# Small expert products scheduled in halves of six matmuls, with new buffer hand-overs and a new order, in a fused attention and two-expert-layer kernel

## The chip, the cores and the metric

The kernel runs on one core of one Trainium2 chip. The metric is the device time of one execution in microseconds, the median of several executions. The engines are called PE (TensorE, matrix products), ACT (ScalarE), DVE (VectorE), POOL (GpSimd) and SP (SyncE, which starts most transfers). SBUF is the on-chip memory, PSUM the banks that PE writes its products to.

## What is computed

Attention of 4 x 8 heads over 576 positions with a decay, then two expert layers on its 2304 tokens of width 512, each with 2048 hidden columns:

```python
scores = scale * np.matmul(q, k.transpose(0, 1, 3, 2))
cum = np.cumsum(np.log(np.clip(f, 0.0001, 1.0)), axis=-1)
scores = np.where(causal, -1e9, scores + cum[..., :, None] - cum[..., None, :])
attn = exp(scores - max) ; attn = attn / (attn.sum(-1) + 1e-09)
x = (attn @ v), heads side by side                      # 2304 x 512
h = x @ w_in ; g = s * relu(h)**2 + b ; x = g @ w_out   # first layer
h = x @ w_in ; g = relu(h) + alpha * min(h, 0) ; out = g @ w_out   # second layer
```

## The kernel before

**Precision.** Matrix products that need it hold each operand as a high and a low part in a float32 form and run three passes: high by high, low by high, high by low (`PASSES`). So one product over 512 rows in chunks of 128 is 4 chunks x 3 passes = 12 matmuls.

**Stages.** Up to about 330 us attention runs beside the first layer's work on token blocks of 256 that are already complete ("small" expert products); from 330 to 590 us the first layer's remaining blocks run in pairs of 512 tokens ("big"); from 590 us the second layer runs, as seven products of blocks in place of eight. In the first stage PE does scores (L906, L907, and L911 for the first heads), transposes of the normalised rows (L1017, L981), value products (L1071), and for each hidden chunk `fc` of 128 the first expert product (L1121: 12 matmuls of 128x256 into bank `h`) and the second (L1153: 12 matmuls from `g` into two `a` banks, six each). Between the two stand ACT (L1131 relu), DVE (L1134 square), ACT (L1138 high part) and DVE (L1144 low part), in the functions `t_a`, `t_b`, `t_c`, `t_d`.

**Around the scores.** DVE masks a score bank and takes its row maximum (L919, followed by a read of an accumulator), ACT forms exponentials with row sums (L924, L927), DVE the reciprocals in two short steps (L931 and L932, or L934), POOL, ACT or DVE the division (L941 and L939). A *turn* is up to four transposes into one of two banks `t`. ACT or DVE evict them (L1026, L1028) into `pt`, from which the value products read; casts to a high part (L1077, ACT or DVE) and a low part (L1082) then make the token block `x`.

**Weights.** Expert weights arrive in packed words, are unpacked on DVE (L534, L537, L540), scaled by ACT (L543) and split into a high part (L560 on ACT, L564 on DVE) and a low part (L563 on POOL), into the tiles `i` (first product) and `o` (second).

**What sets the order.** The program is written as tasks with a list of engines on which each may run, an estimated duration, a priority, the keys it reads and writes, and the ring buffers that it uses. `Scheduler.run` plays these through a small model in time and starts on each engine the ready task with the lowest priority number whose buffers are to be had; the order in which tasks start is the order of the instructions on each engine. The priorities come from the table `PLAN`. A ring hands out a buffer when all users of an earlier one have ended. A *started* task only needs another to have been started ahead of it on the same engine.

**Second layer.** `second_layer` uses banks `h`, `k` and two `a` banks for first products (L1454), copies them out (L1469, L1471, L1492), forms `gq` and `gj` (L1494, L1377, L1379), and runs the second products into four banks `b` (L1392). Differences of token blocks, `xq`, are split on ACT (L1287) and DVE or POOL (L1286) into `xe`.

Of the kernel before, what the change touches and what calls it, by code (L numbers as in the profile page):

```python
# [50 lines left out]
    t0=3.26,  # L51
    ta=0.5395,
    tb=6.6087,
    t1=10.2011,
    t2=15.0154,
    t3=23.3962,
    prep=14.39,
    prepA=208.9144,
    nf=16,
    cp=7.3325,  # L60
    ip=-191.999,
    vp=-7.4436,
    mq=-6.3237,
    grp=4,
    grpA=3,
    max=2.3433,
    pv=3.6414,
    f2=-209.151,
    ap=-11.5752,
    c8=-13.6733,  # L70
    fo=0,
    kp=1,
    at=0,
    nrA='p',
    sc=0,
    wh=4,
    cd=-280.7657,
    ek=0,
    pa=4,
# [4 lines left out]
    xh='va',  # L84
# [3 lines left out]
    cv=(-18.0746, 6.2372, -68.3628, -99.9118, -31.1211, 35.9197, 230.8533, 210.2266, -6.9377, -5.1863, -34.7217, -80.0197, 0.8992, -68.8635, 81.6819, 79.6212),  # L88
    blocks=((-17.7552, 1.8684), (-0.719, 0.903), (0.4402, 2.1001), (1.1144, 1.9861), (1.7724, 2.5485), (2.9671, 3.0)),
# [16 lines left out]
class Buf:  # L106


    def __init__(self, ring):
        self.ring, self.users, self.t = ring, 0, None  # L110
# [16 lines left out]
class Scheduler:  # L127
# [8 lines left out]
    def task(self, opts, r=(), w=(), bufs=(), prio=0.0, started=()):  # L136
# [7 lines left out]
        t.bufs = tuple(bufs)  # L144
# [177 lines left out]
def dv(n):  # L322
    return 70 + 1.035 * n
# [30 lines left out]
def decay_attention_two_moe(ctx: ExitStack, tc: tile.TileContext, qk, qka, v, f, wi1, wo1, wi2, wo2,  # L354
# [14 lines left out]
    def ring(pool, tag, cap, shape, dt):  # L369
        return Ring(cap, lambda n: pools[pool][0].tile(shape, dt, tag=tag, bufs=cap, name=f"{tag}_{n}"))  # L370
# [44 lines left out]
    def o_at(n):  # L415
# [45 lines left out]
        "x": Ring(2, block(lambda i: f"x{i % 2}", "x", 4096 + 16, lambda i: 0 if i < 3 else 16 if i < 7 else 96, [P, KC, 2, T2], lambda i: i if i < 7 else None)),  # L461
# [527 lines left out]
    def transposes(u):  # L989
# [15 lines left out]
        for n, turn in enumerate(turns):  # L1005
            pr = u.t1 + (u.t1 - u.t0) * n / len(turns)
            pp, b0 = R["t"].buf(), 0
            for c, kbs in turn:
# [12 lines left out]
                for x, at, w in outs:  # L1021
                    def t_ev(copy, x=x, at=at, w=w, pp=pp, kbs=kbs, kw=kw, c=c, b0=b0):
# [4 lines left out]
                        else:  # L1027
# [3 lines left out]
                    task(pick(PLAN["ev"], a=("act", ac(nn), lambda f=t_ev: f(nc.scalar.copy)), v=("dve", dv(nn), lambda f=t_ev: f(nc.vector.tensor_copy))),  # L1031
                         r=[(K, "t", part)], w=[((owner, 0, c), "pt", part)], bufs=[pp, x], prio=pr)
                b0 += P * len(kbs)

# [71 lines left out]
    def moe_step(name, fc, x, x0, w, xk, acc, hring, first, last, pr1, pr2, epr, big, half=None):  # L1106
# [9 lines left out]
        def t_mm1():  # L1116
            wv = wi.t.rearrange("p l (k f) -> p l k f", k=KC)
            n = 0
            for kc in range(KC):
                for (wl, xl) in PASSES:  # L1120
                    nc.tensor.matmul(ps.t[:, 0:w], wv[:, wl, kc, :], x.t[:, kc, xl, x0:x0 + w], start=(n == 0), stop=(n == 3 * KC - 1))  # L1121
                    n += 1
# [25 lines left out]
        def t_mm2():  # L1148
            for u in range(KC):
# [8 lines left out]
        if half is None:  # L1158
            mms.append(task(("pe", 12 * mm, t_mm1), r=WK + xk, w=[(K, "h")], bufs=[ps, x, wi], prio=pr1))
# [30 lines left out]
        task(("pe", 12 * mm, t_mm2), r=[(K, "hi"), (K, "lo")] + OK, w=[AK], bufs=[g, wo] + acc, prio=pr2)  # L1190
        return AK

    def finish_pa(blk, acc, AK, epr):

        for i in range(2):
# [3 lines left out]
                 r=[AK, "p1"], w=[("pas", blk, i)], bufs=[acc[i], o], prio=epr)  # L1199
# [43 lines left out]
    def load_x(n, epr):  # L1243

        x = R["x"].buf()
# [9 lines left out]
    def second_layer(order, base, epr):  # L1255
# [3 lines left out]
        xa, xs_, xb = R["x"].buf(), R["xs"].buf(), R["x"].buf()  # L1259
# [7 lines left out]
        for n, (blk, rows) in enumerate(order):  # L1267
# [5 lines left out]
            for i, op in enumerate(XOPS):  # L1273
# [376 lines left out]
    def to_d():  # L1650
# [6 lines left out]
        S5.append(pools["px"][0].tile([P, TH], F32, tag="s5", bufs=1, name="s5_f"))  # L1657
    task(("py", 0.0, to_d), started=mid, w=["px"])
# [61 lines left out]
```

## Time and profile before

| | us |
|---|---|
| median of 3 runs | 947.12 |
| lowest and highest run | 946.66 and 948.70 |
| the profiled execution | 947.46 |
| its span, first to last instruction | 945.7 |
| PE busy | 932.2 |
| DVE, ACT, POOL busy | 711.5, 622.9, 336.6 |

The span is 1.8 us shorter than the profiled execution's own time; that part lies ahead of the first and behind the last instruction. A line such as L1121 is a line of the program before; after the change the same statement stands some 14 to 24 lines further down. PE's records of one operation overlap in the timeline because matmuls are pipelined; the start of the next row, and the idle time in brackets, tell when the engine had nothing to do. The DMA engines are busy 65% of the span, and no wait of PE names them.

### The profile page before, as it was taken

How to read it: one execution, taken by the hardware profiler on the slowest of the kernel's cores; microseconds unless marked ns; L12 is line 12 of the kernel's file. 1: busy time of each engine (PE TensorE's matmuls, PEld its weight loads, DVE VectorE, ACT ScalarE, POOL GpSimd, SP SyncE). 2: the span in 40 equal slices, each digit the busy share in tenths (PEclk: the TensorE clock that was granted, in tenths of full speed). 3: DMA queues.
4: the chain of work that ended last, by engine and by line, in shares of the span. 5: the costliest groups of instructions: out<-in, count | busy, mean ns of one | idle time of the engine just before them, and what ended most of it. 6: DMA issues, size and time to landing. Idle time of an engine off the chain costs nothing.

```text
span 945.7 us, 18349 instructions
## 1 busy us (share of the span) xinstructions
PE 932.2 (99%) x6342; PEld 842.6 (89%) x6342; DVE 711.5 (75%) x1554; ACT 622.9 (66%) x1457; POOL 336.6 (36%) x355
## 2 busy tenths in 40 slices
PE   9999999999999999999999999999999999999997
PEld 7578887999898888988888888999999999999997
DVE  8788858766677556575887675689986869778586
ACT  7799857756677567887777765566654456544552
POOL 7334402422133003577676742133241412523000
PEclk9999999999999999999999999999999999999999
DMA  7856416341534585676979584995698956889566
GB/s 204 268 153 228 148 48 192 124 125 57 189 90 142 179 242 161 226 260 221 361 252 352 198 272 154 352 330 184 188 318 254 320 168 181 254 255 318 164 187 204
DMA packets 99612, 201.41 MB, mean 213 GB/s; under 512 B 10832, under 2 KB 26032, under 8 KB 98880
## 3 DMA queue, kind: packets, MB, share of 16 engines
q1 hardware_dynamic: 99184, 199.78, 65.3%
q8 instruction: 50, 0.82, 0.4%
q10 hardware_dynamic: 336, 0.47, 0.2%
q14 instruction: 42, 0.34, 0.1%
HBM read 146.75 MB, written 50.51 MB: 209 GB/s over the span
## 4 chain that ended last, share of the span: by engine, by line
PE 90%; DVE 5%; ACT 3%; issue 1%; DMA 0%; ACTq 0%; POOL 0%; DVEq 0%; POOLq 0%
PE b L1392 16%; PE h L1121 14%; PE b L1156 9%; PE a L1153 9%; PE a L1454 8%; PE k L1121 6%; PE k L1454 5%; PE h L1454 5%; PE t L1071 4%; PE t L1017 3%; PE s L911 2%; PE a L1156 2%; PE s L906 2%; PE s L907 2%; ACT e L924 1%
## 5 line engine op out<-in xcount | busy, mean ns | idle before, releaser
L1392 PE MATMUL b<-wp,gj 128*128 128x256 f32 x1368 | 172.4, 278 | 0.8 <-DVE gj L1379 0.7
L1392 PEld LDWEIGHTS b<-wp,gj 128*128 128x128 f32 x1368 | 169.4, 188 | 1.2 <-DVE gj L1379 1.0
L1121 PE MATMUL h<-x,i 128*128 128x256 f32 (+1 forms) x864 | 146.4, 318 | 0.2 <-DVE r L1134 0.2
L1121 PEld LDWEIGHTS h<-x,i 128*128 128x128 f32 x864 | 124.4, 188 | 13.2 <-DVE r L1134 0.5
L1379 DVE TENSOR_TENSOR gj<-gq,gj 128x384 fp32r<-128x384 f32 x152 | 100.0, 667 | 31.6 <-ACT gj L1377 31.0
L1377 ACT CAST gj<-gq 128x384 fp32r<-128x384 f32 x142 | 73.0, 515 | 68.5 <-PE b L1392 64.3
L1153 PE MATMUL a<-g,o 128*128 128x256 f32 x768 | 101.3, 281 | 0.0
L1332 POOL TENSOR_TENSOR gq<-gq 128x384 f32<-128x384 f32 x33 | 39.6, 1200 | 162.3 <-DVE gq L1494 141.2
L1153 PEld LDWEIGHTS a<-g,o 128*128 128x128 f32 x768 | 94.7, 188 | 2.4 <-issue 1.0
L924 ACT ACTIVATE e<-e,ngm 128x256 f32<-128x256 f32 (+4 forms) x144 | 83.6, 582 | 19.1 <-DVE ngm L919 17.7
L941 POOL TENSOR_SCALAR e<-e,rec 128x128 f32<-128x128 f32 (+4 forms) x74 | 45.2, 622 | 138.7 <-DVE rec L934 49.1
L1156 PE MATMUL b<-g,o 128*128 128x512 f32 x384 | 93.8, 390 | 0.2 <-POOL g L1175 0.2
L1156 PEld LDWEIGHTS b<-g,o 128*128 128x128 f32 x384 | 71.5, 188 | 14.8 <-POOL g L1175 0.6
L1175 POOL TENSOR_TENSOR g<-r,g 128x512 fp32r<-128x512 f32 (+1 forms) x39 | 53.1, 1364 | 78.4 <-ACT g L1172 73.1
L919 DVE CUSTOM_DVE_ANT_0 e<-s,mask 128x256 f32<-128x256 f32 (+4 forms) x144 | 66.2, 478 | 15.6 <-PE s L907 10.8
L1131 ACT ACTIVATE r<-h 128x256 f32<-128x256 f32 (+1 forms) x76 | 34.0, 448 | 47.1 <-PE h L1121 46.0
L1017 PE MATMUL t<-ident,e 128*128 128x128 f32 (+1 forms) x376 | 54.6, 273 | 3.1 <-ACT pt L1028 2.2
L1454 PE MATMUL h<-x,wq 128*128 128x384 f32 x288 | 57.6, 335 | 0.0
L1017 PEld LDWEIGHTS t<-ident,e 128*128 128x128 f32 (+1 forms) x376 | 43.2, 139 | 11.9 <-issue 3.6
L534 DVE TENSOR_SCALAR cv<-raw 128x512 int32<-128x512 int32 x48 | 25.4, 528 | 37.2 <-ACT raw L543 28.3
L1454 PEld LDWEIGHTS h<-x,wq 128*128 128x128 f32 x288 | 49.4, 188 | 0.2
L1071 PE MATMUL t<-pt,v 128*64 128x320 f32 (+3 forms) x416 | 48.0, 368 | 0.3 <-ACT pt L1028 0.3
(197 smaller groups left out, 2020.2 us busy)
## 6 DMA issues: line engine op xcount, KB each, us to landing
wp<-w2o_d SPq DMA_DIRECT2D x168, 256.0 KB
wq<-w2i_d SPq DMA_DIRECT2D x112, 256.0 KB
raw<-in_wi_dram SPq DMA_DIRECT2D x29, 512.0 KB
w2o_d<-wq SPq DMA_DIRECT2D x56, 256.0 KB
w2i_d<-wq SPq DMA_DIRECT2D x56, 256.0 KB
raw<-in_wo_dram SPq DMA_DIRECT2D x27, 512.0 KB
rawqk<-in_qk_dram SPq DMA_DIRECT2D x20, 576.0 KB
v<-in_v_dram SPq DMA_DIRECT2D x20, 320.0 KB
```

The source lines that it names most:

```text
L919: nc.vector.tensor_tensor_reduce(e.t[0:rows, s0 + k0:s0 + k1], st_.t[0:rows, s0:s0 + w], mask[0:rows, m0:m0 + w], -0.125 if u.f32 else -1. ...
L924: nc.scalar.activation(x, x, AF.Exp, bias=ng[0:rows, col:col + 1], scale=-1.0, accum_out=sm[0:rows, col:col + 1])
L1017: nc.tensor.transpose(pp.t[0:kw, b0 + i * P:b0 + i * P + P], e.t[:, P * kb:P * kb + kw], ident)
L1071: nc.tensor.matmul(o.t[64 * j:64 * j + 64, a - q0:z - q0], vb.t[0:kr, kb, j, :], uu.pt[jj].t[0:kr, kb * step + a:kb * step + z], start=(i ...
L1121: nc.tensor.matmul(ps.t[:, 0:w], wv[:, wl, kc, :], x.t[:, kc, xl, x0:x0 + w], start=(n == 0), stop=(n == 3 * KC - 1))
L1153: nc.tensor.matmul(acc[u // 2].t[:, T * (u % 2):T * (u % 2) + T], wo.t[:, wl, u * P:u * P + P], g.t[:, gl, g0:g0 + w], start=(first and i ...
L1156: nc.tensor.matmul(acc[u].t[:, 0:w], wo.t[:, wl, u * P:u * P + P], g.t[:, gl, 0:w], start=(first and i == 0), stop=end)
L1175: eng.tensor_tensor(g.t[:, 1, g0:g0 + w], r_of(), g_hi().bitcast(F32), ALU.subtract)
L1377: task([("act", ac(TH, False), lambda g=g, qv=qv: nc.scalar.copy(g.t[:, 0, :], qv())), ("dvp", dv2(TH), lambda g=g, qv=qv: nc.vector.tenso ...
L1379: task(("dvp", dv(TH), lambda g=g, qv=qv: nc.vector.tensor_tensor(g.t[:, 1, :], qv(), g.t[:, 0, :].bitcast(F32), ALU.subtract)), r=[("G", ...
L1392: nc.tensor.matmul(y[t // 2].t[:, T * (t % 2):T * (t % 2) + T], g.t[:, gl, t * P:t * P + P], wop[k].t[:, wl, :], start=(fresh and k == 0 a ...
L1454: nc.tensor.matmul(b.t[:, 0:TH], wb.t[:, wl, k * P:k * P + P], x[:, k, xl, :], start=(start and m == 0), stop=(m == 5), skip_group_check=True)
```

## The change

1. **Halves.** A small product of a block of 256 tokens was one task of 12 matmuls. Each is now two tasks of six: the first product by chunks 0 and 1, then 2 and 3; the second product by its two `a` banks. The second task of a pair needs the first to have been started, and the scheduler may put other work between. The eviction of an `a` bank (`finish_pa`) waits for its own half.
2. **Turns.** The evictions of a turn were scheduled each when its own transposes were done; now they are scheduled when all transposes of the turn are done.
3. **Room of the token blocks.** The ring of two `x` buffers, one for a pair of blocks, becomes three: `x0` and `x0b`, which are the two halves of the first pair's buffer, and `x1`. Blocks 4 and 5 take over the room of blocks 0 and 1 one at a time. `Buf.more` lets a task that uses a whole pair count on both halves.
4. **Second layer.** The `xe` tiles are set up at one point, and the first step's casts into them get the lower urgency `epr + 0.5`, so that the copy out of bank `k` can come first.
5. **Order.** Nearly all numbers of `PLAN` are new: how groups of scores are formed (`grp`, `grpA`), when each stage's work falls due, and which engines may run some small steps.

```diff
 PLAN = dict(
-    grp=4,
-    grpA=3,
+    grp=2,
+    grpA=4,
-    pa=4,
+    pa=0,
-    nrA='p',
+    nrA='pv',
-    xh='va',
+    xh='a',
...
-        t.bufs = tuple(bufs)
+        t.bufs = tuple(bufs) + tuple(m for b in bufs for m in b.more if m not in bufs)
...
-        "x": Ring(2, block(lambda i: f"x{i % 2}", "x", 4096 + 16, ...)),
+    R["x0"] = Ring(1, x_even)
+    R["x0b"] = Ring(1, lambda n: xt[0] if n < 2 else "-")
+    R["x1"] = Ring(1, lambda n: x_of(2 * n + 1))
...
-                    task(pick(PLAN["ev"], a=..., v=...),
-                         r=[(K, "t", part)], w=[((owner, 0, c), "pt", part)], bufs=[pp, x], prio=pr)
+                    later.append((t_ev, nn, x, ((owner, 0, c), "pt", part)))
+                keys.append((K, "t", part))
                 b0 += P * len(kbs)
+            for t_ev, nn, x, key in later:
+                task(pick(PLAN["ev"], a=..., v=...),
+                     r=keys, w=[key], bufs=[pp, x], prio=pr)
...
-                X[blk] = R[{0: ...
+                X[blk] = R[{0: "x0", 1: "x0b", 2: "x1", 4: "x0", 5: "x0b", 6: "x1", 8: "xs"}[blk]].buf()
...
-            mms.append(task(("pe", 12 * mm, t_mm1), r=WK + xk, w=[(K, "h")], bufs=[ps, x, wi], prio=pr1))
+            if big:
+                task(("pe", 12 * mm, t_mm1), r=WK + xk, w=[(K, "h")], bufs=[ps, x, wi], prio=pr1)
+            else:
+                a = task(("pe", 6 * mm, lambda: t_mm1(range(0, 2))), r=WK + xk, w=[(K, "h0")], bufs=[ps, x, wi], prio=pr1)
+                task(("pe", 6 * mm, lambda: t_mm1(range(2, 4))), r=WK + xk, w=[(K, "h")], bufs=[ps, x, wi], prio=pr1, started=[a])
...
-        task(("pe", 12 * mm, t_mm2), r=[(K, "hi"), (K, "lo")] + OK, w=[AK], bufs=[g, wo] + acc, prio=pr2)
+        a = task(("pe", 6 * mm, lambda: t_mm2(range(0, 2))), r=[(K, "hi"), (K, "lo")] + OK, w=[(AK, 0)], bufs=[g, wo, acc[0]], prio=pr2)
+        task(("pe", 6 * mm, lambda: t_mm2(range(2, 4))), r=[(K, "hi"), (K, "lo")] + OK, w=[(AK, 1)], bufs=[g, wo, acc[1]], prio=pr2, started=[a])
...
-                 r=[AK, "p1"], w=[("pas", blk, i)], bufs=[acc[i], o], prio=epr)
+                 r=[(AK, i), "p1"], w=[("pas", blk, i)], bufs=[acc[i], o], prio=epr)
...
-                     w=[("xslot", i)], bufs=[b, xq], prio=pr)
+                     w=[("xslot", i)], bufs=[b, xq], prio=epr + 0.5 if n == 0 and i >= 5 else pr)
...
         S5.append(pools["px"][0].tile([P, TH], F32, tag="s5", bufs=1, name="s5_f"))
+        for n in range(NXE):
+            S5.append(pools["px"][0].tile([P, 2, 2, TH], F32R, tag=f"xe{n}", bufs=1, name=f"xe{n}_0"))
```

PE, the first small expert products, about 36 to 41 us of before. In the rows `h`, `s`, `t` and `a` are PSUM banks, `i` and `o` weight tiles, `lkx` the keys and queries of the first heads, `e` normalised rows, with running numbers behind the names. Before:

```order
L1121 MATMUL h_600<-x_428,i_0_501 128x256 x12
L911 MATMUL s_629<-lkx_326 128x384
L1017 MATMUL t_632<-ident,e_2_540 128x128 x4
L1017 MATMUL t_640<-ident,e_2_540 64x128
L1017 MATMUL t_640<-ident,e_4_553 128x128 x3
L1017 MATMUL t_658<-ident,e_4_564 128x128 x4
L911 MATMUL s_671<-lkx_326 128x512
```

Now:

```order
L1145 MATMUL h_505<-x_418,i_0_469 128x256 x3
L925 MATMUL s_587<-lkx_300 128x512
L1031 MATMUL t_592<-ident,e_3_530 128x128 x3
L1031 MATMUL t_600<-ident,e_3_543 128x128 x4
L1145 MATMUL h_505<-x_418,i_0_607 128x256 x3
L1171 MATMUL a_627<-g_612,o_0_564 128x256 x6
L925 MATMUL s_640<-lkx_325 64x288
```

The row of twelve is now two rows of three that stand apart, each on a different weight tile, with a score and seven transposes between; a half of a second product follows where transposes stood.

PE, the middle of attention, about 151 to 155 us of before (`pt` are evicted transposes, `v` values). Before:

```order
L906 MATMUL s_2159<-ka_2070,hq_2073 128x512
L907 MATMUL s_2159<-lk_2059 128x512
L1017 MATMUL t_2165<-ident,e_9_2056 128x128 x4
L1017 MATMUL t_2177<-ident,e_9_2056 64x128
L1017 MATMUL t_2177<-ident,e_18_2108 128x128 x3
L1017 MATMUL t_2194<-ident,e_7_2103 128x128
L1017 MATMUL t_2194<-ident,e_7_2105 128x128 x2
L1017 MATMUL t_2201<-ident,e_18_2127 128x128 x4
L1071 MATMUL t_2213<-pt_2117,v_1882 64x256
```

Now:

```order
L920 MATMUL s_2187<-ka_1843,hq_1872 64x288
L921 MATMUL s_2187<-lk_1841 64x288
L1140 MATMUL h_2199<-x_418,i_0_1506 128x256 x12
L1171 MATMUL a_2059<-g_2196,o_0_1500 128x256 x6
L1171 MATMUL a_2081<-g_2196,o_0_1500 128x256 x6
L920 MATMUL s_2239<-ka_1992,hq_2003 128x256
L921 MATMUL s_2239<-lk_1990 128x256
L1091 MATMUL t_2243<-pt_1968,v_1728 64x256
```

Before, a value product follows fifteen transposes; now twelve matmuls of a first product and two sixes of a second stand ahead of it instead, with a score between.

ACT at the start of the second layer, about 587 to 595 us of before, with the numbers of the tiles (`g2_55` is the first layer's last operand, `k_28`, `a_22`, `a_18`, `h_77`, `h_76` are banks). Before:

```order
L1172 ACTIVATE g2_55_7325<-r2_55_7232 128x512
L1287 CAST xe0_0_7386<-xq_0_6122 128x2x384
L1287 CAST xe1_0_7388<-xq_0_6122 128x2x384
L1471 COPY s5_f_7385<-k_28_7276 128x384
L1471 COPY u2_0_7398<-a_22_7270 128x384
L1492 ACTIVATE gq_0_7406<-h_77_7245,as_t_133 128x384
```

Now:

```order
L1194 ACTIVATE g2_55_7380<-r2_55_7286 128x512
L1494 COPY s5_f_7431<-k_28_7328 128x384
L1494 COPY u2_0_7435<-a_18_7318 128x384
L1515 ACTIVATE gq_0_7439<-h_76_7292,as_t_133 128x384
L1310 CAST xe0_0_7432<-xq_0_6157 128x2x384
L1310 CAST xe1_0_7433<-xq_0_6157 128x2x384
```

The two casts into `xe0` and `xe1` moved from ahead of the copies `s5_f` and `u2_0` to behind `gq_0`. PE at the same place, from the last row of the first layer, before:

```order
L1156 MATMUL b_11_7060<-g2_55_7325,o7_0_5935 128x512 x3
L1454 MATMUL k_28_7276<-xe0_0_7386,wq_90_7148 128x384 x6
L1454 MATMUL a_22_7270<-x_8_7230,wq_89_7145 128x384 x6
L1454 MATMUL h_77_7245<-x_7_6830,wq_91_7236 128x384 x6
L1454 MATMUL a_22_7270<-xe1_0_7388,wq_86_7089 128x384 x6
```

Now:

```order
L1174 MATMUL b_11_7095<-g2_55_7380,o7_0_6008 128x512 x3
L1477 MATMUL a_18_7318<-x_8_7284,wq_89_7191 128x384 x6
L1477 MATMUL h_76_7292<-x_7_6897,wq_91_7244 128x384 x6
L1477 MATMUL k_28_7328<-xe0_0_7432,wq_90_7199 128x384 x6
L1477 MATMUL a_19_7478<-xs_1_6989,wq_95_7362 128x384 x6
```

Bank `k` with `xe0` came first behind the first layer's last row; now bank `a` and bank `h`, each with a block that is not an `xe`, come ahead of it.

## Rows read from the trace of the kernel before

**Rows 1.** the page's busy times: engine, busy us (share of the span), instructions

```profile
PE 932.2 (99%) x6342; PEld 842.6 (89%) x6342; DVE 711.5 (75%) x1554; ACT 622.9 (66%) x1457; POOL 336.6 (36%) x355
```

**Rows 2.** busy us by stretch: length, each engine (instructions), clock, DMA

```profile
40.00:100.00 60.00, 59.24 (x415) 42.41 (x413) 51.10 (x146) 55.67 (x151) 22.23 (x20) 1.00 0.62 194
...
100.00:330.00 230.00, 226.82 (x1840) 202.59 (x1839) 164.98 (x511) 156.50 (x462) 60.02 (x90) 1.00 0.40 127
...
590.00:946.00 356.00, 349.59 (x2510) 348.09 (x2509) 280.55 (x529) 188.66 (x371) 88.99 (x78) 1.00 0.76 245
```

**Rows 3.** PE's waits: line <- what ended it: us, times, longest

```profile
PE s L911 <- DVE ngm L919: 2.4, 3, 1.3
PE t L1017 <- ACT pt L1028: 2.2, 4, 0.9
PE k L1454 <- ACT s_f L1471: 1.3, 1, 1.3
```

**Rows 4.** PE in order: start, us, operation, [idle before <- what ended it]

```profile
139.37 0.63 PE L1017 MATMUL t<-ident,e 128*128 128x128 f32 x4 [0.33 <-ACT pt L1028]
...
154.04 1.07 PE L1017 MATMUL t<-ident,e 128*128 128x128 f32 x7 [0.74 <-DVE pt L1028]
155.38 3.07 PE L1071 MATMUL t<-pt,v 128*64 128x256 f32 x28 [0.27 <-ACT pt L1028]
```

**Rows 5.** the same view, 36 to 50 us

```profile
36.91 0.91 PE L911 MATMUL s<-lkx 66*128 66x384 f32 x2 [0.52 <-DVE ngm L919]
...
39.27 0.63 PE L1017 MATMUL t<-ident,e 128*128 128x128 f32 x4 [0.58 <-ACT pt L1028]
...
49.02 1.19 PE L1121 MATMUL h<-x,i 128*128 128x256 f32 x8 [0.24 <-DVE r L1134]
```

**Rows 6.** the same view, 237 to 241 us

```profile
239.42 0.55 PE L1017 MATMUL t<-ident,e 128*128 128x128 f32 x3 [0.88 <-ACT pt L1028]
240.38 0.63 PE L1017 MATMUL t<-ident,e 128*128 128x128 f32 x4 [0.41 <-ACT pt L1028]
```

**Rows 7.** the chain that ended last: start, us, PE's expert matmuls

```profile
118.04 1.36 PE h L1121 x12
...
120.87 1.42 PE h L1121 x12
...
158.45 1.58 PE h L1121 x12
```

**Rows 8.** groups by shape, 0 to 330 us: busy, mean ns | idle before

```profile
L1134 DVE SCALAR_TENSOR_TENSOR r<-h,small,r 128x256 f32<-128x256 f32 x48 | 23.0, 479 | 16.1 <-ACT r L1131 15.6
...
L563 POOL TENSOR_TENSOR i<-cv,i 128x512 fp32r<-128x512 f32 x8 | 10.6, 1326 | 4.8 <-DVE i L564 3.4 <-ACT i L560 1.4
...
L931 DVE TENSOR_SCALAR rec<-sums 128x4 f32<-128x4 f32 x16 | 2.7, 168 | 7.9 <-ACT e L924 7.9
```

**Rows 9.** the start of the second layer, PE, ACT and POOL in order

```profile
594.47 1.31 PE L1454 MATMUL k<-xe,wq 128*128 128x384 f32 x6 [1.30 <-ACT s_f L1471]
...
593.21 0.83 ACT L1287 CAST xe<-xq 128x768 fp32r<-128x768 f32 x1 [1.89 <-PE b L1156]
...
594.69 0.59 ACT L1492 ACTIVATE gq<-h,as_t 128x384 f32<-128x384 f32 x1
...
594.12 1.85 POOL L1286 TENSOR_TENSOR xe<-xq,xe 128x768 fp32r<-128x768 f32 x1 [9.79 <-DVE F L1232]
```

**Rows 10.** DVE and POOL in order, 577 to 585 us

```profile
577.33 2.10 DVE L607 TENSOR_TENSOR sw<-cf 128x256 f32<-128x256 f32 x1
...
584.80 0.41 DVE L607 TENSOR_TENSOR sw<-sw,cf 128x256 f32<-128x256 f32 x1
...
577.29 1.86 POOL L1279 TENSOR_TENSOR xq<-xq 128x768 f32<-128x768 f32 x1 [11.79 <-DVE x L1286]
```

**Rows 11.** busy us by stretch, as rows 2, up to two points

```profile
0.00:95.10 95.10, 91.56 (x627) 66.40 (x627) 81.32 (x244) 79.07 (x227) 43.02 (x62) 1.00 0.73 213
...
0.00:127.30 127.30, 122.68 (x870) 93.98 (x870) 104.32 (x305) 103.08 (x294) 53.09 (x74) 1.00 0.63 186
```

More of the change, by code (lines that the diff above doesn't have):

```diff
@@ L50 @@
 PLAN = dict(
[L51 to L58, printed above, removed]
-    nf=16,
[L60 to L63, printed above, removed]
-    grp=4,
-    grpA=3,
[L66 to L73, printed above, removed]
-    nrA='p',
-    sc=0,
+    t0=10.1481,
+    ta=0.01,
+    tb=5.7489,
+    t1=11.8834,
+    t2=12.0484,
+    t3=23.1511,
+    prep=14.9068,
+    prepA=128.7213,
+    nf=16,
+    cp=-1.5867,
+    ip=-128.1395,
+    vp=7.0286,
+    mq=-2.0659,
+    grp=2,
+    grpA=4,
+    max=13.3232,
+    pv=4.7504,
+    f2=-111.2113,
+    ap=-4.992,
+    c8=-16.2337,
+    fo=1,
+    kp=9,
+    at=7500.0,
+    nrA='pv',
+    sc=4,
     wh=4,
-    cd=-280.7657,
-    ek=0,
-    pa=4,
+    cd=-180.575,
+    ek=2,
+    pa=0,
     tA=-90.0,
@@ L109, in __init__ @@
     def __init__(self, ring):
-        self.ring, self.users, self.t = ring, 0, None
+        self.ring, self.users, self.t, self.more = ring, 0, None, []
 class Ring:
@@ L1006, in transposes @@
             pr = u.t1 + (u.t1 - u.t0) * n / len(turns)
-            pp, b0 = R["t"].buf(), 0
+            pp, b0, later, keys = R["t"].buf(), 0, [], []
             for c, kbs in turn:
@@ L1030, in transposes @@
                     owner = U if at or c < 4 else u.mate.i
[L1031 to L1032 removed]
+                    later.append((t_ev, nn, x, ((owner, 0, c), "pt", part)))
+                keys.append((K, "t", part))
                 b0 += P * len(kbs)
+            for t_ev, nn, x, key in later:
+                task(pick(PLAN["ev"], a=("act", ac(nn), lambda f=t_ev: f(nc.scalar.copy)), v=("dve", dv(nn), lambda f=t_ev: f(nc.vector.tensor_copy))),
+                     r=keys, w=[key], bufs=[pp, x], prio=pr)
     X = {}
@@ L1114, in moe_step, with t_mm1 @@
         mm = MM[w]
-        def t_mm1():
+        def t_mm1(kcs=range(KC)):
             wv = wi.t.rearrange("p l (k f) -> p l k f", k=KC)
[L1118 to L1122, printed above, removed]
+            for kc in kcs:
+                for n, (wl, xl) in enumerate(PASSES):
+                    nc.tensor.matmul(ps.t[:, 0:w], wv[:, wl, kc, :], x.t[:, kc, xl, x0:x0 + w], start=(n == 0 and kc == 0), stop=(n == 2 and kc == KC - 1))
         def t_chunk(kc):
@@ L1146, in moe_step, with t_mm2 @@
         g0 = (123, 111)[fc % 2] if big and w == T else 0
-        def t_mm2():
-            for u in range(KC):
+        def t_mm2(us=range(KC)):
+            for u in us:
                 for i, (wl, gl) in enumerate(PASSES):
@@ L1243, in load_x @@
     def load_x(n, epr):
-        x = R["x"].buf()
+        x = R["x1"].buf() if n == 1 else whole()
         blks = [2 * n, 2 * n + 1]
@@ L1258, in second_layer @@
         bank = {"Z": R["h"].buf(), "X": R["k"].buf(), "W0": R["a"].buf(), "W1": R["a"].buf()}
-        xa, xs_, xb = R["x"].buf(), R["xs"].buf(), R["x"].buf()
+        xa, xs_, xb = R["x1"].buf(), R["xs"].buf(), whole()
         xe = [R[f"xe{n}"].buf() for n in range(NXE)]
```

23 lines of the change are left out of this document (17 added, 6 removed).

## The prediction

> **What bounds the kernel now.** I read the busy shares first: TensorE (PE) works 932.2 of 945.7 us of the span [rows 1], so it is the bound from end to end, and no other engine exceeds 75%. The granted clock is 1.00 in each stretch [rows 2], the higher level (2.4 GHz), so nothing is to be had from the clock. The change leaves the number of PE instructions as it is, so only two things can move the time: the 13.5 us in which PE does nothing (945.7 - 932.2), and what a passage from one kind of matmul to another costs within its busy time. The second view to read is therefore PE busy by stretch. Between 100 and 330 us, where attention and the small expert products share PE, it is idle 3.2 us (230.0 - 226.82); between 40 and 100 us 0.8 (60.0 - 59.24); between 590 and 946 us 6.4 (356.0 - 349.59), most of that the tail of the kernel, which the change does not touch [rows 2]. The third view names who is waited for: 2.4 us of score products for the mask reduction on VectorE (DVE), 2.2 us of transposes for an ACT eviction of the turn before, 1.3 us once at the start of the second layer [rows 3]. DVE and ScalarE (ACT) are busy 165 and 157 us of the 230 between 100 and 330 us [rows 2]; they do not bound, they only come late at single places. So at most some 5 us of waits lie in the stretch that the change reorders, and the question is which of them go and which come back.
>
> **The change part by part.** The sum is made against the profiled execution's own 947.46 us, of which 945.7 are span. It lies 0.34 above the median of 947.12.
>
> *Waits that go (the middle of attention).* At 152 to 155 us fifteen transposes stand in a row in before's order, with the value product behind them; the two transpose banks are full, and PE waits 0.74 us for a DVE eviction and 0.27 for an ACT one; 0.33 was lost in the same way at 139 us [rows 4]. In the changed order scores and a small expert product with its two half products stand there instead, so that 24 expert matmuls (some 2.7 us by [rows 7]) cover the evictions. I take all three away: -1.34.
>
> *A wait that is replaced (the first small expert products, 36 to 49 us).* Before waits 0.52, 0.58 and 0.24 there, 1.34 in all [rows 5]. The new order puts two rows of three matmuls early, the second on a weight tile (i_0_607) whose preparation stands late on DVE: behind a relu step that itself waits for the first product, then a cast on DVE, then the low part on GpSimd (POOL). PE has nothing but one score of 512 columns (one of 384 took 0.91 [rows 5]) and seven transposes (1.07 [rows 4]) in between, 1.9 us since they overlap, to lay beside about 3.2 us: the ACT and DVE steps of the relu 1.4 (0.48 each and the hand-overs), the cast 0.5, taken as long as such a step, the low part 1.3 [rows 8]. Estimate of the wait: 3.2 - 1.9 = 1.3, so the place as a whole comes to 0. Bounds: -1.34 if the cast is early enough, +0.5 if a DVE step more lies in front.
>
> *A wait that stays.* At 237 to 241 us runs of three and of four transposes wait 0.88 and 0.41 us for ACT, and a value product follows them [rows 6]. The new order has four runs of transposes (3, 4, 4, 4) and then the value product at the same point of PE's work: no cover has been added. Evicting a whole turn after its last transpose makes the first eviction of a turn start up to three transposes later (seven in a row took 1.07 [rows 4], so 3 x 0.15 at most), and I put +0.2 on it (0 to 0.45). At about five smaller places, too, the new order leaves PE one or two pieces of work between a transpose or a reduction and its reader, against two or three before; each I price at half of the smallest listed waits (0.24 to 0.33 [rows 4, 5]), 0.12: +0.6 (0 to 1.5).
>
> *Passages between kinds of matmul.* A row of twelve expert matmuls costs 1.36 us behind other expert matmuls, 1.42 behind a transpose, 1.58 behind a value product [rows 7]: +0.06 and +0.22 a passage. By counting the order, passages from transposes to expert, score or value products go from 59 to 71, and from value products to expert or score products from 24 to 28: 12 x 0.06 + 4 x 0.22 = 1.6. In some of them a shorter piece hides part; bounds 0.6 to 1.6, taken 1.0.
>
> *Halves of six.* In the changed order 47 of the second products still run as a row of twelve and only 22 as rows of six; for the first products it is 83 of twelve, 19 of six, 6 of three. The weights, the banks and the counts are the same, so a half that is not separated costs nothing. Nothing is priced beyond the passages above.
>
> *Whole-turn evictions, room handed on by halves, small norms.* The reordering of groups gives DVE 16 more of each of the two short steps for the row sums (0.168 us [rows 8] and taken as long, so 32 x 0.168 = 5.4 us), and 17 casts go from DVE to ACT. Both have 65 us or more of slack between 100 and 330 us [rows 2], which hides these as sums. The half buffers give the first token pair's room back earlier; no PE wait of before is on that room, so 0. If that cover were gone, it would be the DVE queue below.
>
> *Start of the second layer.* PE ends the first layer's last 24 matmuls at about 593.2 and waits 1.30 us, for one copy out of bank k [rows 9]; that copy stands on ACT behind the cast of xe (593.21, 0.83). In the new order the copy of s5 comes ahead of the casts, but PE's own order starts with bank a: it waits for the copy of u2, which now lies over a tile that the last matmul reads, so it can't start ahead of 593.2 either. In before, 0.43 us lay between the end of the last cast (594.04) and PE's start, which the copy of k took [rows 9]; with a hand-over from PE to ACT ahead of it, the first group starts some 0.55 late. The second needs bank h: gq on ACT 0.59 [rows 9], then on DVE about as long, some 0.15 beyond the cover. The third needs xe0, whose high cast now comes after gq (594.3 to 595.1), and whose low part POOL takes 1.85 us for [rows 9], to 596.9: about 0.6 beyond PE's two groups of six, of about 1.1 us each (one took 1.31 to its last end [rows 9]). Sum 0.55 + 0.15 + 0.6 = 1.3, what it was: 0. Bounds: -1.3 if all three overlap, +0.8 below. On DVE, subtractions of 128x256 took 2.10 us while POOL ran on a tensor of its own, and 0.41 later with POOL idle [rows 10]; a DVE subtraction of gj now stands beside POOL's 1.85, and if it is held for most of that, the release of the next bank is 0.8 later. The Trainium skill ("SBUF — State Buffer", section "SBUF: two separate sides") has it that DVE with two SBUF inputs and GpSimd take a shared port pair by an exclusive lock held for a whole instruction; by that rule the subtraction would wait for all of POOL's step, and this place would cost the +0.8. The trace agrees in kind: 2.10 against 0.41.
>
> *Sum.* 947.46 - 1.34 + 0 + 0.2 + 0.6 + 1.0 + 0 = 947.9; less 0.34 for where the median lies: **947.5 us**.
>
> **The rivals.** *Faster: the waits of stage A go and none comes back.* For it: they total some 5 us up to 330 us (3.2 and 0.8 by stretch, 0.52 and 0.58 just ahead of 40 us), nearly all for ACT or DVE, which are 28% idle there or more, and finer pieces give a scheduler more to lay between. If all but 0.9 us go (-4.0) and passages cost 1.0, the result is 947.12 - 4.0 + 1.0 = 944.1. Against it: the places read above, where the new order has as little cover as the old. Half of it, 945.5, would be within what can be told from no change.
>
> *Slower: the DVE queue takes over.* At the point of PE's work that before reaches at 127.3 us DVE was busy 104.32 us [rows 11], idle 23.0. In the new order more DVE work stands ahead of the work that PE waits for at that point: ten more reductions with their reads, nine more evictions, seven norms that POOL had, six more low parts, less five casts and five steps of expert relus; at the durations of their shapes about +8.4 us, nearly all between 100 and 127 us. So DVE may be idle only 23.0 - 8.4 = 14.6 us up to there. It had been idle 13.8 by 95.1 us already (95.1 - 81.32) [rows 11]; if it keeps a third or more of the other 9.2 (reductions that wait for scores), 13.8 + 3.1 - 14.6 = 2.3 us pass to PE, at a half 3.8. It decides from 14.6 us of idle DVE. Time: 947.5 + 2.3 to 3.8 = 949.8 to 951.3; taken 950.0, near the lower end since the lead is short. For it: reductions are already the largest wait of PE (2.4 [rows 3]). Against it: at 95 and at 139 us of PE work the lead is only about 1 us, and scores that come earlier let DVE work earlier.
>
> *The change does not do what it says.* Halves run back to back in most places (47 against 22), so the finer tasks may do next to nothing, and only the new order is left. That gives no measurable change too, and is inside the forecast.
>
> **How the numbers follow.** A measurement of this kernel tells about 0.2%, 1.9 us, from no change: 945.2 to 949.0. The bounds of the terms around 947.5: below -1.34 (first products), -1.3 (second layer), -0.8 (small returns and the turn) make 944.1 if all came together, and two of the three about 945.3; above +0.5, +0.9, +0.6 and +0.8 make 950.3, and two of them about 949. So the forecast's own range is 945.3 to 949.0, with a chance of 0.42; the faster rival 0.34, the slower one 0.24. A range that holds 8 in 10 reaches from just below the faster rival's 944.1, 943.6, to just above the slower one's 950.0, 950.6. Chances: faster 0.34, same 0.42, slower 0.24.
>
> **What would show it.** Right: PE's busy time rises by about 1 us while its idle time stays at 12.5 to 13.5; the list of waits keeps transposes on ACT at about 239 us, loses those at 139 and 154 us, has a new wait of an expert product on a weight tile's low part from POOL near 40 us, and three short waits near 593 us in place of the one of 1.30. Wrong on the fast side: less than 2.5 us of idle PE between 30 and 330 us, or a first group near 593 with no wait behind it. Wrong on the slow side: scores that wait for reductions between 100 and 130 us with DVE over 90% busy there. A busy time of PE that did not rise would refute the passages; one that rose by over 2 us would make me wrong on the slow side through them.

## The result, and the profile after

The changed kernel takes 951.38 us (median of 7 runs, 951.26 to 957.09) against 947.12 before; the ratio over all runs is 1.0052, with an interval of 1.0039 to 1.0066 (the medians alone give 1.0045). It is slower by some 4.3 us; the forecast was 947.5, in a range that ended at 950.6. The profiled execution took 951.38 us, with a span of 949.6. Four of the seven runs, those with a mean granted clock of 0.999 or 1.000, took 951.26 to 951.38; the other three, at 0.993 to 0.998, took 952.32 to 957.09.

The busy times first, in the same form as [rows 1], and PE's waits as in [rows 3]; both of the changed kernel:

```profile
PE 936.5 (99%) x6342; PEld 846.5 (89%) x6342; DVE 722.3 (76%) x1577; ACT 622.8 (66%) x1474; POOL 341.4 (36%) x363
```

```profile
PE s L925 <- DVE ngm L933: 2.1, 2, 1.1
PE t L1031 <- DVE pt L1042: 1.9, 3, 0.8
...
PE h L1140 <- POOL i L577: 0.7, 1, 0.7
PE h L1145 <- POOL i L577: 0.7, 1, 0.7
PE a L1477 <- ACT u L1494: 0.6, 1, 0.6
PE k L1477 <- POOL xe L1309: 0.4, 1, 0.4
```

PE's idle time went down, from 13.5 to 13.1 us (949.6 - 936.5). Its busy time went up, from 932.2 to 936.5, with the same 6342 records. So the loss is no wait. Where it arises is told by the start of the same operation in both kernels. The timeline of PE, before and then after (start us, us, operation; the first row of before shows eleven of its twelve matmuls):

```profile
331.51 2.65 PE L1121 MATMUL h<-x,i 128*128 128x512 f32 x11
...
456.80 2.92 PE L1121 MATMUL k<-x,i 128*128 128x512 f32 x12
...
610.18 1.20 PE L1454 MATMUL k<-xe,wq 128*128 128x384 f32 x6
...
940.19 1.52 PE L1392 MATMUL b<-wp,gq 128*128 128x256 f32 x12
```

```profile
331.08 2.88 PE L1140 MATMUL h<-x,i 128*128 128x512 f32 x12
...
456.92 2.92 PE L1140 MATMUL k<-x,i 128*128 128x512 f32 x12
...
610.90 1.20 PE L1477 MATMUL k<-xe,wq 128*128 128x384 f32 x6
...
944.16 1.53 PE L1415 MATMUL b<-wp,gq 128*128 128x256 f32 x12
```

The differences are -0.43, +0.12, +0.72 and +3.97 us. Attention, which the change reorders, gained 0.4; something in the first layer's big products took back 0.55; the start of the second layer took 0.6; and between 610 and 940 us, where both kernels run the same rows on PE in the same order, 3.25 us were lost a little at a time. Busy time and number of instructions from 700 to 800 us, before and after:

```profile
700.00:800.00 100.00, 100.00 (x725) 100.00 (x724) 77.82 (x141) 55.03 (x108) 27.44 (x26) 1.00 0.74 235
```

```profile
700.00:800.00 100.00, 100.00 (x718) 100.00 (x717) 76.53 (x140) 53.50 (x103) 27.55 (x26) 1.00 0.75 236
```

PE is 100% busy in both, at the same granted clock, but it does 725 matmuls in one and 718 in the other. The groups by shape name them: the second products of the second layer, before and after.

```profile
L1392 PE MATMUL b<-wp,gj 128*128 128x256 f32 x1368 | 172.4, 278 | 0.8 <-DVE gj L1379 0.7
```

```profile
L1415 PE MATMUL b<-wp,gj 128*128 128x256 f32 x1368 | 175.5, 281 | 0.7 <-DVE gj L1402 0.7
```

172.4 against 175.5 us for 1368 matmuls of one shape; the products of 384 columns beside them (L1454, L1477) differ by under 0.3 us a group. From start to start, one of the 1366 undisturbed ones took 116.25 ns before and 118.45 after, on average: 1366 x 2.2 ns = 3.0 us. Split by operand, 2.90 of the 3.25 us arise in the rows on `gj` and 0.35 in the products of 384 columns between them.

What differs for these matmuls is where their operand `gj` lies. The tiles of a pool are laid out in the order in which the program first asks for each kind. `c22` (1984 bytes) and the four `gj` tiles (3584 each) are both asked for first at the start of the second layer. Before, `c22` came first, and the first `gj` tile starts at byte 144,864; after, `gj` comes first and starts at 142,880. Part 4 of the change is enough to exchange them (part 1 alone or the new table alone would do so too). The streamed operand `wp` lies where it lay, and the other operands that PE reads from SBUF keep their places modulo 256 bytes.

### The profile page after: what moved, and what is told of

Its sections match the earlier page's. It is cut to its first block, busy times and chain, and to the rows that moved or that the text cites. A ratio compares the mean times of both kernels' runs of the same rounds, so it can differ in the third digit from the quotient of the medians.

```text
span 949.6 us, 18428 instructions
## 1 busy us (share of the span) xinstructions
PE 936.5 (99%) x6342; PEld 846.5 (89%) x6342; DVE 722.3 (76%) x1577; ACT 622.8 (66%) x1474; POOL 341.4 (36%) x363
## 4 chain that ended last, share of the span: by engine, by line
PE 90%; DVE 5%; ACT 2%; DMA 1%; issue 1%; POOL 0%; DVEq 0%; SPq 0%; ACTq 0%
PE b L1415 18%; PE h L1140 14%; PE a L1171 8%; PE b L1174 8%; PE a L1477 8%; PE k L1140 6%; PE k L1477 5%; PE h L1477 5%; PE t L1091 5%; PE t L1031 4%; PE s L925 3%; PE a L1174 2%; PE s L920 2%; PE s L921 2%; DMA raw<-in_wo_dram 1%
## 5 line engine op out<-in xcount | busy, mean ns | idle before, releaser
L1415 PE MATMUL b<-wp,gj 128*128 128x256 f32 x1368 | 175.5, 281 | 0.7 <-DVE gj L1402 0.7
L1415 PEld LDWEIGHTS b<-wp,gj 128*128 128x128 f32 x1368 | 171.9, 188 | 1.1 <-DVE gj L1402 0.9
L938 ACT ACTIVATE e<-e,ngm 128x128 f32<-128x128 f32 (+4 forms) x144 | 83.7, 583 | 23.5 <-DVE ngm L933 21.2
L955 POOL TENSOR_SCALAR e<-e,rec 128x128 f32<-128x128 f32 (+4 forms) x74 | 48.0, 652 | 139.4 <-DVE rec L946 74.8
L1197 POOL TENSOR_TENSOR g<-r,g 128x512 fp32r<-128x512 f32 (+1 forms) x36 | 47.1, 1309 | 100.1 <-ACT g L1194 98.8
L933 DVE CUSTOM_DVE_ANT_0 e<-s,mask 128x128 f32<-128x128 f32 (+4 forms) x144 | 65.8, 478 | 10.6 <-PE s L921 8.4
L548 DVE TENSOR_SCALAR cv<-raw 128x512 int32<-128x512 int32 x48 | 30.4, 634 | 36.8 <-ACT raw L557 28.1
L1477 PE MATMUL h<-x,wq 128*128 128x384 f32 x288 | 57.8, 336 | 0.0
L1091 PE MATMUL t<-pt,v 128*64 128x320 f32 (+4 forms) x432 | 50.2, 367 | 0.1
L1091 PEld LDWEIGHTS t<-pt,v 128*64 128x64 f32 (+1 forms) x432 | 27.0, 135 | 25.7 <-issue 5.0
```

Source lines behind the costliest of these rows:

```text
L933: nc.vector.tensor_tensor_reduce(e.t[0:rows, s0 + k0:s0 + k1], st_.t[0:rows, s0:s0 + w], mask[0:rows, m0:m0 + w], -0.125 if u.f32 else -1. ...
L938: nc.scalar.activation(x, x, AF.Exp, bias=ng[0:rows, col:col + 1], scale=-1.0, accum_out=sm[0:rows, col:col + 1])
L955: eng.tensor_scalar(x, x, rc[0:rows, col:col + 1], 1.0, ALU.mult, ALU.mult)
L1091: nc.tensor.matmul(o.t[64 * j:64 * j + 64, a - q0:z - q0], vb.t[0:kr, kb, j, :], uu.pt[jj].t[0:kr, kb * step + a:kb * step + z], start=(i ...
L1415: nc.tensor.matmul(y[t // 2].t[:, T * (t % 2):T * (t % 2) + T], g.t[:, gl, t * P:t * P + P], wop[k].t[:, wl, :], start=(fresh and k == 0 a ...
L1477: nc.tensor.matmul(b.t[:, 0:TH], wb.t[:, wl, k * P:k * P + P], x[:, k, xl, :], start=(start and m == 0), stop=(m == 5), skip_group_check=True)
```

## The experiments

The theory was that the exchange of addresses makes the loss, and everything else nearly cancels. The rival was that the pace of PE follows from what the other engines do beside it in the new order. Four kernels tell these apart, against 947.39 us for the kernel before on the same chip.

**The changed kernel, `c22` asked for ahead of `gj`.**

```diff
+    def gj_at(n):
+        if n == 0 and not C22:
+            c22_at(0)
+        return pools["px"][0].tile([P, 2 * TH + 128], F32R, tag="gj", ...)
```

> The changed kernel with one thing put back: the tile c22 is laid out ahead of the four gj tiles, as in the kernel before; in the changed kernel gj lies ahead of c22, 1984 bytes lower. Order and work are those of the changed kernel. Theory (addresses): the second products of the second layer read gj at addresses that make each of their 1366 matmuls about 2 ns slower, 3.3 us of the 4.3 us; put back, about 948.1 us, and these matmuls busy 172.4 us in place of 175.5. Rival (the pace comes from what other engines do beside PE in the new order): unchanged, 951.4 us and 175.5 us.

Measured: 948.84 us (10 runs), ratio 1.0021 (1.0008 to 1.0034), and the second products are back at their pace:

```profile
L1426 PE MATMUL b<-wp,gj 128*128 128x256 f32 x1368 | 172.4, 278 | 0.8 <-DVE gj L1413 0.7
```

The span of the profiled run is 946.2, 3.4 us less than the changed kernel's, and the lag behind the kernel before stays at +0.54 from 611 to 941 us. By the medians 2.5 us of the 4.3 came back. The spread of the ten runs goes with the granted clock: the five at a mean of 0.999 or 1.000, the profiled one among them, took 948.0 to 948.4, the other five, at 0.993 to 0.998, 949.2 to 953.9. Against the runs of the changed kernel at 0.999 or 1.000 (951.3) some 3.1 us came back, near the 3.3 of the theory. What PE did before the clock fell in those five isn't shown.

**The kernel before, `gj` views moved by 64 bytes.** No instruction changes its place in the order.

```diff
-... tag="gj", bufs=4, name=f"gj_{n}")[:, 2:2 + 2 * TH]
+... tag="gj", bufs=4, name=f"gj_{n}")[:, 18:18 + 2 * TH]
```

> The kernel before with its instructions unchanged, only the start of each gj view moved from 2 to 18 words into its tile, so that its place modulo 128 bytes is that of the changed kernel (40 in place of 104). Theory (addresses): 947.1 + 3.2 = 950.3 us, second products of the second layer busy 175.5 us. Rival (the order of the other engines' work): unchanged, 947.1 us and 172.4 us. A third result, a rise of another size, would say that the rest of the address counts as well.

Measured: 950.88 us, ratio 1.0042 (1.0028 to 1.0057); `gj` matmuls 175.5 us. The loss is made in the old kernel by the address alone, and the rival falls. (Its profiled run took 953.36; it lost another 2.4 us ahead of 56 us. There PE waited 1.76 us for a reduction at 38.1 us, in place of 0.52, and behind that wait the granted clock was at its lower level, 1.2 GHz, for most of the stretch from 39.0 to 42.6 us, 0.53 on average. The lag that grows between 611 and 941 us is 3.26, as in the changed kernel.)

**Part 4 alone, with the addresses that follow from it, and with the old ones.**

```diff
-                     w=[("xslot", i)], bufs=[b, xq], prio=pr)
+                     w=[("xslot", i)], bufs=[b, xq], prio=epr + 0.5 if n == 0 and i >= 5 else pr)
...
+        for n in range(NXE):
+            S5.append(pools["px"][0].tile([P, 2, 2, TH], F32R, tag=f"xe{n}", bufs=1, name=f"xe{n}_0"))
```

> The kernel before with part 4 of the change alone: the xe tiles set up early and the first step's casts at the lower urgency, so that the copy out of bank k comes first. The layout of c22 and gj then comes out as in the changed kernel. Theory: this part alone gives nearly the whole loss, 3.3 us by addresses and 0.6 us at the start of the second layer, 951.0 us. Rival (the loss comes from the halves and the new order of attention): about 947.1 us.

> The kernel before with part 4 of the change alone, and c22 laid out ahead of gj as before. What is left is the exchange of short waits at the start of the second layer. Theory: 947.1 + 0.6 = 947.7 us, three short waits of together 1.2 us or more near 594 us in place of one of 1.3. Rival (part 4 as a gain of its own, the wait of 1.3 gone): 945.8 us.

Measured: 950.67 us (ratio 1.0032, 1.0018 to 1.0045) with `gj` at 175.5 us, and 947.75 us (1.0004, 0.9994 to 1.0013) with `gj` at 172.4. So part 4 alone makes 3.3 of the 4.3 us, and nearly all of that by the layout. Its own exchange of waits is worth nothing that can be measured. The start of the second layer in the second of these kernels:

```profile
593.92 1.31 PE L1465 MATMUL a<-x,wq 128*128 128x384 f32 x6 [0.57 <-ACT u L1482]
595.06 1.30 PE L1465 MATMUL h<-x,wq 128*128 128x384 f32 x6
596.92 1.31 PE L1465 MATMUL a<-xs,wq 128*128 128x384 f32 x6 [0.55 <-ACT a L1480]
```

Two waits of together 1.12 us stand in place of the one of 1.30 [rows 9]; three of 1.2 or more were expected.

**The parts of the change for attention,** each with the addresses of the kernel before: the halves alone in the old kernel; the changed kernel with its small products back in tasks of twelve; and the changed kernel with the old table of numbers.

> The kernel before with part 1 of the change alone (small products as tasks of six), its old table of numbers, and c22 laid out ahead of gj so that gj keeps its addresses (with part 1 alone they would have changed places as in the changed kernel). Theory: the halves by themselves neither give nor take more than 1 us, 946.5 to 948.4 us, second products of the second layer at 172.4 us. Rival (finer tasks let the scheduler cover the waits of attention): 944 us, PE idle less than 2.5 us between 40 and 330 us.

> The changed kernel with c22 laid out ahead of gj, and the small products back to tasks of twelve. Against the run with c22 put back alone (948.4 us): theory (the halves count for little), 947.5 to 949.5 us. Rival (the new table of numbers was made for halves, and they cover waits): 950 us or more, with more idle PE between 40 and 330 us.

> The changed kernel with c22 laid out ahead of gj and the old table of numbers: parts 1 to 4 without the new order. Theory: the parts without the order and without the addresses come out near the kernel before, 947.4 us plus the 0.4 us of part 4 measured alone, 947.8 us. Rival (part 2, evictions of whole turns, costs more than 0.2 us a place in before's long rows of transposes): 949 us or more, with longer waits of transposes for evictions than 2.9 us.

Measured, against 947.52 for the kernel before: 958.48 (ratio 1.0118, 1.0103 to 1.0133), 954.31 (1.0080, 1.0063 to 1.0097) and 956.12 (1.0092, 1.0071 to 1.0113). All three expectations of near neutrality missed (the 948.4 that the second starts from is 948.84 by that run's median). The rival of the second (the table was made for halves) came out, and so did the bounds of the third's: 956.12, with waits of transposes for evictions of 3.9 us; but that part 2 makes them isn't shown, since the halves alone lose more. In all three `gj` ran at 172.1 to 172.5 us; most of what they lose is lost by 331 us of before: 8.7, 5.1 and 5.8 us in their profiles. PE busy from 100 to 330 us in the kernel without halves, in the one with halves alone, and in the changed kernel:

```profile
100.00:330.00 230.00, 224.73 (x1818) 199.79 (x1817) 172.50 (x549) 159.55 (x473) 60.96 (x93) 1.00 0.40 125
```

```profile
100.00:330.00 230.00, 222.77 (x1805) 197.79 (x1803) 170.35 (x513) 156.53 (x463) 56.95 (x83) 1.00 0.39 123
```

```profile
100.00:330.00 230.00, 227.41 (x1853) 204.51 (x1852) 165.09 (x524) 158.49 (x473) 60.50 (x89) 1.00 0.39 124
```

The first two idle 5.3 and 7.2 us there, against 3.2 before [rows 2] and 2.6 after; the rest of their loss by 331 us wasn't traced. The table of numbers and the pieces that it orders fit only each other: each loses without the other, and together they come out 0.4 us ahead in one profile, which is within what one profile can tell.

**Which addresses are slow.** The kernel before, with `gj` views starting at other words of their tiles, one profile each. The theories count bytes modulo 128 or 512, the table modulo 256.

> The kernel before, gj views starting at word 0 of their tiles (byte 96 modulo 128, the same as the wp tiles that stream past them). Theory 1 (only the place modulo 128 counts, and 104 is a chosen good place): second products of the second layer slower than 172.4 us. Theory 2 (an equal place of weights and streamed operand is best): 172.4 us or less.

> The kernel before, gj views starting at word 10 (byte 8 modulo 128, 40 bytes past wp's place). If what counts is whether a row of 128 values starts on a boundary of 32 bytes, this is as 2 and 18 words are, off by 8, and the two measured values of 172.4 and 175.5 would not differ; so the place modulo 128 or more must count, and this lies between them or beyond: 172 to 177 us.

> The kernel before, gj views starting at word 26 (byte 72 modulo 128, 104 bytes past wp's place). Same theories as for word 10: 172 to 177 us; with the runs at 2, 10 and 18 words it gives the four places of a period of 128 bytes at steps of 32.

> The kernel before, gj views starting at word 34, that is 128 bytes past the start in the kernel before. Theory 1 (period of 128 bytes): 172.4 us again. Theory 3 (a longer period, 256 or 512 bytes): another value, such as the 175.5 us of word 18.

> The kernel before with gj views starting at word 4 (byte 496 modulo 512, one step of 8 bytes past before's 488 and 16 past wp's 480). Measured so far, second products of the second layer by start modulo 512: 480: 177.0 us, 488: 172.4, 8: 176.1, 40: 175.5, 72: 174.9, 104: 175.1. Theory (a narrow good place just past wp's own): 173 to 175 us. Rival (every place from 488 to 512, whose rows cross a boundary of 512 bytes close to their start, is good): 172.4 us or less.

> The kernel before with gj views starting at word 16, byte 32 modulo 512, a multiple of 32 and the place of the gq tiles, whose matmuls against wp at the end of the kernel took 114.4 ns from start to start, against 116.25 for gj in the kernel before and 118.45 in the changed one. Theory A (place alone sets the pace): gj then runs at 114.4 too, 169.9 us in place of 172.4. Theory B (gq is faster since it stands at the end, where the other engines are done): about 175.5 us as at byte 40.

> The kernel before with gj views starting at word 66, 256 bytes past before's start, byte 232 modulo 512. Theory (the place modulo 512 counts): not 172.4 us but 174 to 177. Rival (modulo 256): 172.4 us.

> The kernel before with gj views starting at word 124, byte 464 modulo 512, 16 bytes ahead of wp's place in place of 8 behind it. Theory (a narrow place just behind wp's own): 174 to 177 us. Rival (any place near the end of a stretch of 512 bytes): 172.4 us or less.

> The kernel before with gj views starting at word 1, byte 484 modulo 512, between 480 (177.0 us) and 488 (172.4). Theory (a narrow good place that begins 4 to 8 bytes behind wp's): 172 to 177 us; a value at 177.0 or at 172.4 says on which side of it the step lies.

| first word of the view | byte modulo 256 | `gj` matmuls, us | lag grown from 611 to 941 us | execution, us |
|---|---|---|---|---|
| 0 | 224 | 177.0 | 5.1 | 953.29 |
| 1 | 228 | 175.6 | 3.4 | 951.21 |
| 2 (before) | 232 | 172.4 | 0 | 947.46 |
| 4 | 240 | 175.5 | 3.5 | 951.11 |
| 10 | 8 | 176.1 | 3.9 | 950.55 |
| 16 | 32 | 174.4 | 3.1 | 950.45 |
| 18 | 40 | 175.5 | 3.3 | 950.88 (median) |
| 26 | 72 | 174.9 | 3.3 | 950.80 |
| 34 | 104 | 175.1 | 2.6 | 949.29 |
| 66 | 232 | 172.5 | 0.1 | 947.20 |
| 124 | 208 | 173.9 | 1.8 | 948.79 |
| 2, `gj` first (after) | 40 | 175.5 | 3.3 | 951.38 (median) |

The lag is that behind the kernel before, between the same two rows of PE as above.

A period of 128 bytes falls with word 34 (175.1); one of 256 fits word 66 (172.5), the one place at which it was tried. That the rest of the address counts isn't borne out either: the changed kernel and word 18 share the place 40 and the pace, 2048 bytes apart. The good place is narrow, between 228 and 240. `wp` lies at 224, so it is 8 bytes behind `wp`'s own. The theory that an equal place is best falls (word 0, 177.0, is the worst). Word 16 fits neither of its theories (169.9 or 175.5), word 4 lies above its 173 to 175, and word 124 just below its 174. No place tried beats the kernel before, and no version was found that beats both kernels. Whether the place itself counts or its distance from `wp` wasn't tried; `wp` can't be moved without moving what lies around it.

A tile's own place isn't all that sets its pace. `gq` lies at byte 32 in the kernel before and at word 16 alike, and at word 16 `gj` has that place too. The group of `gq` in the two kernels:

```profile
L1392 PE MATMUL b<-wp,gq 128*128 128x256 f32 x144 | 17.4, 277 | 0.0
```

```profile
L1392 PE MATMUL b<-wp,gq 128*128 128x256 f32 x144 | 18.0, 282 | 0.0
```

In its longest row, 81 matmuls, `gq` took 113.3 ns from start to start before and 117.8 at word 16, and 117.8 at word 0 as well, though neither `gq` nor `wp` had moved; the products of 384 columns between lost up to 1.0 us (words 16 and 26). So where `gj` starts also changes the pace of other matmuls near those on `gj`; the column of the lag holds all of them. How the pace passes from one row to the next isn't shown.

## Why the prediction was wrong

**The step that failed** is a sentence of the first part: the change leaves the number of PE instructions as it is, "so only two things can move the time", idle time and passages between kinds of matmul. There is a third: the pace of one matmul at unchanged order, clock and count. It moved by 2.2 ns, 1366 times. No term of the sum had it, none of the rivals had it, and it is nearly the whole of the miss: 947.5 + 3.25 = 950.75, already beyond the upper end of 950.6. The diff showed new code for the place of tiles (`S5.append` for `xe`), and I read it for waits alone. The built programs state each tile's address before any run; comparing them would have shown that `gj` moved, though no row of the kernel before gives the price of such a move.

**The slower rival had the sign, not the mechanism;** that the result lies next to its 949.8 to 951.3 is a coincidence. Its premise held nearly to the digit. DVE's busy time up to 127.3 us (the same time, not the same point of PE's work), as in [rows 11], in the changed kernel:

```profile
0.00:95.10 95.10, 91.11 (x613) 65.03 (x614) 83.37 (x254) 77.30 (x232) 46.57 (x66) 1.00 0.72 218
95.10:127.30 32.20, 31.48 (x245) 26.62 (x246) 29.54 (x91) 29.34 (x98) 14.21 (x18) 1.00 0.37 114
0.00:127.30 127.30, 122.59 (x857) 91.66 (x859) 112.91 (x344) 106.63 (x328) 60.79 (x84) 1.00 0.63 192
```

112.91 against 104.32 is +8.6 us, where +8.4 was worked out. But DVE was idle 11.7 us up to 95.1 in place of the 13.8 that I carried over, and 2.7 of the 9.2 behind it, 92% busy; that makes 14.4, inside the 14.6 at which it was to decide. PE paid one wait of 0.72 at 105.86 us, for an eviction; no score waited for a reduction there. Idle time of an engine ahead of a bottleneck moves with the order; it isn't a fixed price to carry over.

**Attention** was put at +0.5 us (-1.34 + 0 + 0.2 + 0.6 + 1.0) and came to -0.43. PE's busy time in this stage, from the first row that starts at the same time in both kernels, before and after:

```profile
12.64:330.00 317.36, 312.32 (x2431) 263.35 (x2432) 239.66 (x741) 233.57 (x689) 95.52 (x130) 1.00 0.48 150
```

```profile
12.65:329.57 316.92, 312.26 (x2431) 263.80 (x2432) 242.71 (x767) 233.59 (x707) 99.36 (x134) 1.00 0.47 148
```

The waits: -0.54 forecast, -0.38 measured (5.04 to 4.66). The three at 139 to 155 us are gone, as forecast. Near 40 us there is the new wait on the weight's low part from POOL, and another one for a reduction. These two, and those at 239 us:

```profile
35.21 1.12 PE L925 MATMUL s<-lkx 66*128 66x512 f32 x2 [1.09 <-DVE ngm L933]
...
37.90 0.50 PE L1145 MATMUL h<-x,i 128*128 128x256 f32 x2 [0.68 <-POOL i L577]
...
236.86 1.23 PE L1031 MATMUL t<-ident,e 128*128 128x128 f32 x8 [0.39 <-DVE pt L1042]
238.88 0.63 PE L1031 MATMUL t<-ident,e 128*128 128x128 f32 x4 [0.79 <-DVE pt L1042]
```

0.68 against the 1.3 of the estimate, half of it; with the 1.09 the place comes to +0.43, where 0 was forecast and +0.5 was the bound. The place at 239 us keeps its waits (0.39 + 0.79 against 1.29 in [rows 6]), now for DVE, as forecast without the 0.2. The passages were the mis-sized term: +1.0 forecast, and -0.06 measured (312.32 to 312.26). Counted in the traces, those from transposes (L1017) went from 75 to 85, where the prediction has 59 to 71, and those from value products to expert or score products from 23 to 26, where it has 24 to 28; at its prices that makes 1.26 in place of 1.6. The prediction named a rise of PE's busy time by over 2 us as the sign that its passages were too low; it rose by 4.3, and none of that rise lies in attention. All of this is close to what one profile can tell: ten profiles with before's order differ by -0.83 to +0.78 us between 84 and 124 us alone, where a weight transfer ends, one of them by 2.4 ahead of 56.

**A wait that I did not price,** 0.68 at 446 us against 0.18 at 442 before, in a stage where the sum had nothing:

```profile
444.63 1.36 POOL L577 TENSOR_TENSOR i<-cv,i 128x512 fp32r<-128x512 f32 x1 [0.39 <-ACT i L574]
...
446.05 1.20 PE L1140 MATMUL h<-x,i 128*128 128x512 f32 x4 [0.68 <-POOL i L577]
```

The new order leaves a later weight's low part to POOL just ahead of its use. These two waits make 0.50 of the +0.55 between 331 and 457 us.

**The start of the second layer** was put at 0 with bounds -1.3 and +0.8, and cost 0.60. Its steps came as worked out: 0.57 for the copy of u2 (0.55 forecast), nothing for bank h (0.15), 0.43 for POOL's low part of xe (0.6), 1.0 in place of 1.3. PE in order, after:

```profile
593.86 1.32 PE L1477 MATMUL a<-x,wq 128*128 128x384 f32 x6 [0.57 <-ACT u L1494]
595.02 1.29 PE L1477 MATMUL h<-x,wq 128*128 128x384 f32 x6
596.15 0.51 PE L1477 MATMUL k<-xe,wq 128*128 128x384 f32 x2
...
600.37 1.32 PE L1477 MATMUL a<-xe,wq 128*128 128x384 f32 x6 [0.23 <-DVE c L1498]
```

Two things turned this small gain into a loss. One is the mechanism of the upper bound. POOL and DVE in order:

```profile
595.15 4.02 POOL L1309 TENSOR_TENSOR xe<-xq,xe 128x768 fp32r<-128x768 f32 x2 [10.13 <-ACT xe L1310]
```

```profile
595.38 2.08 DVE L1402 TENSOR_TENSOR gj<-gq,gj 128x384 fp32r<-128x384 f32 x1
597.38 2.47 DVE L1255 TENSOR_TENSOR F<-b,F 128x512 f32<-128x512 f32 x4
599.77 0.54 DVE L1498 TENSOR_TENSOR c<-a,s_f 128x384 f32<-128x384 f32 x1
```

The subtraction of `gj` took 2.08 us beside POOL where the mean of its group is 0.66, so by the order of DVE's rows the step that frees bank a came late, and PE waited once more, 0.23 at 600.37. With it the idle time comes to 1.23, still under the 1.30 of before. So the other thing decides: each new stop costs more than the idle time shown. Rows of six that follow one another start 1.04 us apart, but 1.16 and 1.13 after the first stop, and there are three stops in place of one.

So the sum, with everything that the profiles show: -0.43 + 0.55 + 0.60 + 3.25 = 3.97 us, against a span that grew by 3.9.

## What to carry to other kernels

When a change adds, removes or merely reorders the first use of tiles, compare the address of every tile that the matmuls read, before and after, as one compares the order of instructions; a tile that moved is a change of its own, and here the dearest. In a trace, a busy share of 100% says nothing of pace: compare how many instructions of a shape go through in an equal stretch, or their mean duration. And pin the layout of tiles whose place was tuned, by asking for them in a fixed order, so that a change elsewhere can't move them.

## What the runs showed of the hardware

In kernels that differ in nothing but where the stationary operand `gj` starts within 256 bytes, its 128x256 matmuls with float32 operands in high and low parts took 116.25 to 119.6 ns from start to start on average, at the same granted clock. 232 was the one good place among the ten tried, 8 bytes behind the place of the streamed operand. The order of the other engines' work isn't the cause: the slow and the fast pace appear with the instructions of all engines in the same order. The effect reaches further than the moved tile: matmuls on `gq`, whose place stayed, took 113.3 or 117.8 ns in their longest row. Why the chip does so, and whether accesses of other engines have a part in it, isn't shown by any run here.

A DVE subtraction of 128x384 took 2.08 us beside a POOL step on other tiles, against 0.66 in the mean of its group. The rule of the Trainium skill that the prediction weighed ("SBUF — State Buffer", section "SBUF: two separate sides": an exclusive lock of the port pair that both share) fits these rows; the wait of PE that stands behind it was 0.23 us, less than the 0.8 that went with the rule.
